# The last layer's tokens: 32x32 blocks and VectorE transposes in place of TensorE transposes

## The chip, the core and the metric

One core of one Trainium2 chip runs the whole program in one launch. The metric is the device time of an execution in microseconds (us); three executions of the kernel before were timed, and one more was taken by the hardware profiler.

## The reference

```
x = attention(q, k, v, beta)          # delta-rule state, 4 x 8 heads, 768 steps
x = moe(x, ...)                       # 3072 tokens, top-1 of 8 experts, D=384, F=1024
h = x @ w_in                          # 3072 x 384 by 384 x 2048
g = h * (1.0 / (1.0 + np.exp(-h)))
return (g @ w_out).astype(np.float32) # 2048 x 384
```

The change is in the last three lines, the dense layer ("Ffn" in the kernel). `w_in` and `w_out` arrive as 64-bit floats and are unpacked on the chip.

## The kernel before, in words

**Stages.** Attention and routing take about the first 310 us, the experts the next 220, the last layer the rest, from about 529 us of the span. The stages overlap at their edges: one scheduler puts the instructions of the whole program in order, engine by engine, by times that it works out itself; the code's `issue_after` gives it lower bounds. Each engine then runs its own list strictly in order, and SP's list holds nearly all DMAs.

**Experts (L1252, L1259).** The experts write their rows to a DRAM tensor `ys` (3072 x 384) by scatters from GpSimd. In the last slot of the experts each of eight pieces of the hidden dimension is a first product `ph` (nine matmuls), an activation that ScalarE writes and VectorE corrects (`pairs`, L1409 and L1410), and a second product `poe` of twelve matmuls: high by high, high by low, low by high, for four blocks of tokens. The weights of each piece are split into a high and a low part by ScalarE (L1215) and VectorE (L1216): `wRH` for the first product, `w2s` for the second.

**Last layer (`Ffn`).** Tokens are worked on in six groups of 512. `tokens(g)` (L1606) loads a group's 512 rows of `ys` into the tile `fy` (128 partitions, 4 blocks of 128 tokens, 384 features) by one DMA on SP (L1609), and turns them so that features lie on partitions: for each of three blocks k of 128 features, four TensorE transposes of 128x128 into one PSUM tile `fpt` (L1613), a cast to the high part `fxh` on ScalarE (L1614) and the low part `fxl` on VectorE (L1615). Two buffers of `fy` alternate; the second one, `fy2`, lies in memory that the experts' raw weights use until the last of them is split. `tokens(0)` is called in the experts' last slot, `tokens(g + 1)` in group g after its ninth piece.

`group(g)` (from L1618) goes through 16 pieces f of 128 hidden features: the first product `fph` (L1629, nine matmuls of 128x512), the sigmoid on ScalarE (L1632), the gated value gv on VectorE (L1634, written to a part of `fy2`'s memory, so the profile calls it fy), its high part gh on ScalarE (L1636, fgh) and its low part gl on VectorE (L1638, fq), and one piece later the second product `fpo` (L1646, twelve matmuls of 128x384). Within the first group the rest of `w_out` is still loaded (L1507, tiles `ro8` to `ro15`, two buffers) and unpacked by ScalarE and VectorE (L1518 to L1527). After 16 pieces the result goes out through `ob` (L1672, L1676).

PSUM has eight banks: five under the tag "pa", of which two hold the third and fourth block of a group's result and three go round between `fph` and `fpt`.

Of the kernel before, what the change touches and what calls it, by code (L numbers as in the profile page):

```python
# [715 lines left out]
class Router:  # L716
# [210 lines left out]
    def finish(self, n):  # L927
# [109 lines left out]
        def spots():  # L1037
            pd, ps = pick(self.pd), new("ps", [128, NT])
            if n == 0:
                u = tokens("u", v["w"], 2)  # L1040
                tt(ps, pd, u[:, 1], op=ALU.add)
                left = new("left", [128, NT])
                tt(left, pd, u[:, 0], op=ALU.is_ge)
                stt(ps, left, -1024.0, ps, op0=ALU.mult, op1=ALU.add)
            else:
                u = tokens("u", v["w"], 4)
                j, f = new("j", [128, NT]), new("f", [128, NT])
                tt(j, pd, u[:, 0], op=ALU.subtract)
                tt(ps, j, u[:, 2], op=ALU.add)
                tt(f, j, u[:, 1], op=ALU.is_ge)  # L1050
                tt(f, f, u[:, 3], op=ALU.mult)
                tt(ps, ps, f, op=ALU.add)
                nc.vector.tensor_scalar(f, j, 0.0, -1024.0, op0=ALU.is_lt, op1=ALU.mult)
                tt(ps, ps, f, op=ALU.add)
            v["ps"] = ps
# [475 lines left out]
class Ffn:  # L1531
# [74 lines left out]
    def tokens(self, g):  # L1606
        nc, P = self.nc, self.P
        xh, xl, y = self.take("xh"), self.take("xl"), self.take("y")
        nc.sync.dma_start(y, self.ys.rearrange("(t b p) d -> t p b d", b=4, p=128)[(g + 3) % 6])  # L1609
        for k in range(3):  # L1610
            pt = P["pa"].tile([128, 512], F32, tag="pa", name=f"fpt{g}_{k}")
            for c in range(4):
                nc.tensor.transpose(pt[:, 128 * c : 128 * c + 128], y[:, c, 128 * k : 128 * k + 128], self.ident)  # L1613
            nc.scalar.copy(xh[:, k, :], pt)  # L1614
            nc.vector.tensor_tensor(xl[:, k, :], pt, xh[:, k, :], op=ALU.subtract)  # L1615
        return xh, xl
# [222 lines left out]
```

## Time and profile before

| | before |
|---|---|
| median of 3 runs | 941.42 us (940.8 to 942.2) |
| the profiled execution | 947.22 us |
| its span, first to last instruction | 945.5 us |
| TensorE busy | 894.5 us, 95% |
| VectorE busy | 573.5 us, 61% |
| ScalarE busy | 429.3 us, 45% |
| DMA traffic | 85.27 MB in 68583 packets |

A row of the profile names a line of the kernel (L1613), an engine (PE is TensorE's matmul, PEld its weight load, DVE VectorE, ACT ScalarE, POOL GpSimd, SP the engine that issues DMAs), an operation and the tiles it writes and reads (out<-in). Busy times of TensorE's pipelined matmuls overlap a little, so the distance from one start to the next says more than a matmul's own duration. The profiled execution is longer than the median of the timed runs by 5.8 us.

### The profile page before, as it was taken

To read this page: it belongs to the slowest core of one execution; us is meant where nothing else is said; L and a number is where in the kernel's file an instruction comes from. 1 tells how busy PE (TensorE), PEld (TensorE's weight loads), DVE (VectorE), ACT (ScalarE), POOL (GpSimd) and SP (SyncE) were. 2 spreads that over 40 slices of the span, in tenths; PEclk is the share of its full clock that TensorE was granted. 3 is DMA by queue.
4 is the path that set the end of the run, shared out by engine and by line. 5 is a ranking of instruction groups with operands and counts; after the bars stand their busy time and mean duration, and the time that the engine had idled before them with its cause. 6 is when DMAs were issued, how large, how long until landed. Compare 5 with 4: busy or idle time off the path is not lost. (4 is left out here: it accounts for less than half of the span.)

```text
span 945.5 us, 23368 instructions
## 1 busy us (share of the span) xinstructions
PE 894.5 (95%) x9605; PEld 781.0 (83%) x9605; DVE 573.5 (61%) x1648; ACT 429.3 (45%) x842; POOL 83.7 (9%) x85
## 2 busy tenths in 40 slices
PE   7779998977999799999989999999999999999997
PEld 4449898876888577889878899898999999999997
DVE  4999898989924693699954556433333333343332
ACT  4127576853776434466643544333332332332332
POOL 5000000011011244122211100000000000000000
PEclk9897999988999999999999999999999999999999
DMA  8932746635154505576641312000010000000000
GB/s 199 176 102 73 171 106 167 163 86 185 34 142 116 176 22 171 172 233 197 214 145 58 104 50 68 34 2 33 34 34 1 34 1 1 34 1 1 34 0 34
DMA packets 68583, 85.27 MB, mean 90 GB/s; under 512 B 29961, under 2 KB 54679, under 8 KB 68464
## 3 DMA queue, kind: packets, MB, share of 16 engines
q1 hardware_dynamic: 65136, 73.83, 28.3%
q0 software_dynamic: 3328, 9.83, 3.1%
q8 instruction: 78, 1.28, 0.6%
q14 instruction: 41, 0.34, 0.1%
HBM read 70.53 MB, written 14.55 MB: 90 GB/s over the span
## 5 line engine op out<-in xcount | busy, mean ns | idle before, releaser
L1646 PE MATMUL fpo<-o,fgh 128*128 128x384 f32 x768 | 184.3, 338 | 0.0
L1634 DVE TENSOR_TENSOR fy<-fph,fy 128x512 f32<-128x512 f32 x96 | 66.4, 691 | 161.8 <-ACT fy L1632 161.3
L1646 PEld LDWEIGHTS fpo<-o,fgh 128*128 128x128 f32 x768 | 139.3, 188 | 7.9 <-ACT fgh L1636 0.4
L1632 ACT ACTIVATE fy<-fph 128x512 f32<-128x512 f32 x96 | 57.4, 598 | 169.4 <-PE fph L1629 166.6
L1646 PE MATMUL fpo<-o,fq 128*128 128x384 f32 x384 | 116.6, 338 | 0.0
L1629 PE MATMUL fph<-fxh,ih 128*128 128x512 f32 x288 | 113.7, 395 | 0.0
L1629 PE MATMUL fph<-fxh,il 128*128 128x512 f32 x288 | 113.2, 393 | 0.0
L1638 DVE TENSOR_TENSOR fq<-fy,fgh 128x512 fp32r<-128x512 f32 x96 | 66.4, 692 | 74.4 <-ACT fgh L1636 63.3
L1636 ACT CAST fgh<-fy 128x512 fp32r<-128x512 f32 x96 | 59.7, 622 | 80.4 <-DVE fy L1634 44.6
L1259 PE MATMUL poe<-w2s,pairs 128*128 128x384 f32 x384 | 77.5, 344 | 3.9 <-ACTq L1490 3.2
L1259 PEld LDWEIGHTS poe<-w2s,pairs 128*128 128x128 f32 x384 | 69.2, 191 | 8.0 <-ACTq L1490 3.5
L1646 PEld LDWEIGHTS fpo<-o,fq 128*128 128x128 f32 x384 | 71.1, 188 | 0.5
L416 DVE TENSOR_TENSOR tmp<-A,L 128x126 f32<-128x126 f32 (+20 forms) x336 | 70.7, 252 | 0.9
L422 DVE TENSOR_TENSOR A<-A,tmp 128x126 f32<-128x126 f32 (+20 forms) x336 | 70.5, 251 | 0.0
L1252 PE MATMUL bank<-xh,wRH 128*128 128x256 f32 x240 | 61.3, 332 | 6.6 <-DVE wRH L1308 6.0
L1629 PEld LDWEIGHTS fph<-fxh,il 128*128 128x128 f32 x288 | 54.1, 188 | 9.7
L1629 PEld LDWEIGHTS fph<-fxh,ih 128*128 128x128 f32 x288 | 54.1, 188 | 9.0
L1346 PE MATMUL po<-raw,hs 128*128 128x384 f32 x160 | 60.4, 501 | 0.0
L1629 PE MATMUL fph<-fq,ih 128*128 128x512 f32 x144 | 56.9, 395 | 0.0
L1629 PE MATMUL fph<-fxl,ih 128*128 128x512 f32 x144 | 56.5, 392 | 0.0
L1252 PEld LDWEIGHTS bank<-xh,wRH 128*128 128x128 f32 x240 | 41.6, 199 | 11.8 <-DVE wRH L1308 6.8
L709 PE MATMUL po<-ones 128*128 128x512 bf16 x103 | 32.9, 432 | 14.1 <-DVE KB L347 6.8
(432 smaller groups left out, 1587.2 us busy)
## 6 DMA issues: line engine op xcount, KB each, us to landing
raw<-in_moe_w_dram SPq DMA_DIRECT2D x72, 384.0 KB
ri<-in_moe_w_in_dram SPq DMA_DIRECT2D x12, 512.0 KB
ro<-in_moe_w_out_dram SPq DMA_DIRECT2D x16, 384.0 KB
vs<-in_vd_dram SPq DMA_DIRECT2D x12, 384.0 KB
KI<-in_kd_dram SPq DMA_DIRECT2D x24, 192.0 KB
Z<-vs SPq DMA_DIRECT2D x24, 192.0 KB
xs<-Y SPq DMA_DIRECT2D x48, 96.0 KB
fy<-ys SPq DMA_DIRECT2D x6, 768.0 KB
```

The lines of the kernel that those rows point to most:

```text
L416: nc.vector.tensor_tensor(tv, r[:, :, j : j + 1].to_broadcast([128, c, n]), L[:, j : j + 1, j + 1 :].to_broadcast([128, c, n]), op=ALU.mult,)
L422: nc.vector.tensor_tensor(r[:, :, j + 1 :], r[:, :, j + 1 :], tv, op=ALU.add)
L709: return nc.tensor.matmul(room, dense, dense[:, None, :].to_broadcast([128, 4, 128]), start=True, stop=True).ins
L1252: self.nc.tensor.matmul(ph, a[:, k, :], b[:, k, :], start=(i == 0), stop=(i == 8))
L1259: self.mark = self.nc.tensor.matmul(o, a[:, cs], b, start=(c == 0 and i == 0), stop=(c == self.F - 1 and i == 2)).ins
L1346: nc.tensor.matmul(self.po[b][:, 0:384], v["h"][c % 2][:, 128 * b : 128 * b + 128], self.raw(1, c), start=(c == 0), stop=(c == F - 1),)
L1629: nc.tensor.matmul(ph, a[:, k, fs], b[:, k, :], start=(n == 0), stop=(n == 8))
L1632: nc.scalar.activation(sg, ph, AF.Sigmoid)
L1634: nc.vector.tensor_tensor(gv, ph, sg, op=ALU.mult)
L1636: self.marks = [nc.scalar.copy(gh, gv).ins]
L1638: self.marks.append(nc.vector.tensor_tensor(gl, gv, gh, op=ALU.subtract).ins)
L1646: nc.tensor.matmul(po[c], a[:, rows], b, start=(f == 0 and i == 0), stop=(f == 15 and i == 2))
```

## The change

Only `tokens` changes. The one DMA of a group becomes twelve, for four ranges i of 32 features and three blocks k: each brings, for 32 partitions, 16 pieces of 32 floats, so that partition 32i + p holds, for each of 16 runs n of 32 tokens, 32 features of token 32n + p. A block transpose of 32x32 on VectorE then gives, in one instruction for each k, what four TensorE transposes gave. The casts that follow stay; their lines move from L1614 and L1615 to L1619 and L1620, and all later lines by 5.

```diff
     def tokens(self, g):
         nc, P = self.nc, self.P
         xh, xl, y = self.take("xh"), self.take("xl"), self.take("y")
-        nc.sync.dma_start(y, self.ys.rearrange("(t b p) d -> t p b d", b=4, p=128)[(g + 3) % 6])
+        blocks = self.ys.rearrange("(t n p) (k i d) -> t i p k n d", n=16, p=32, k=3, i=4)[(g + 3) % 6]
+        y = y.rearrange("p b d -> p (b d)").rearrange("p (k n) -> p k n", k=3)
+        for i in range(4):
+            for k in range(3):
+                nc.sync.dma_start(
+                    y[32 * i : 32 * i + 32, k].rearrange("p (n d) -> p n d", d=32), blocks[i, :, k]
+                )
         for k in range(3):
             pt = P["pa"].tile([128, 512], F32, tag="pa", name=f"fpt{g}_{k}")
-            for c in range(4):
-                nc.tensor.transpose(pt[:, 128 * c : 128 * c + 128], y[:, c, 128 * k : 128 * k + 128], self.ident)
+            nc.vector.transpose(out=pt, in_=y[:, k])
             nc.scalar.copy(xh[:, k, :], pt)
             nc.vector.tensor_tensor(xl[:, k, :], pt, xh[:, k, :], op=ALU.subtract)
         return xh, xl
```

The scheduler gives the new program another order in the last slot of the experts and in the last layer. VectorE, last slot of the experts (`wRH` and `w2s` are low parts of weights, `pairs` low parts of activations, the number in `ph_12_4` is the piece), as a difference:

```order
 L1216 TENSOR_TENSOR wRH<-raw_4193,wRH 128x384
+L1618 STREAM_TRANSPOSE fpt_0_12019<-fy 128x512
 L1410 SCALAR_TENSOR_TENSOR pairs<-ph_12_4_11908,pairs 128x512
-L1216 TENSOR_TENSOR w2s<-raw_4284,w2s 128x384
+L1618 STREAM_TRANSPOSE fpt_1_12023<-fy 128x512
+L1620 TENSOR_TENSOR fxl<-fpt_0_12019,fxh 128x512
+L1216 TENSOR_TENSOR w2s<-raw_4284,w2s 128x384
+L1618 STREAM_TRANSPOSE fpt_2_12027<-fy 128x512
+L1620 TENSOR_TENSOR fxl<-fpt_1_12023,fxh 128x512
 L1216 TENSOR_TENSOR wRH<-raw_4193,wRH 128x384
 L1410 SCALAR_TENSOR_TENSOR pairs<-ph_12_5_11943,pairs 128x512
```

The three transposes of the first group stand ahead of, or between, the pairs of pieces 4 and 5; before, VectorE's first work on these tokens stood behind the pairs of piece 6. On ScalarE the casts `fxh` move up in the same way, the second one ahead of a weight cast and the pairs of piece 5.

TensorE at the same place, in the changed program, with what each row waits for (Activation is ScalarE):

```order
L1259 MATMUL poe_12_7568<-w2s,pairs 128x384 [waits Activation_49]
L1259 MATMUL poe_12_7568<-w2s,pairs 128x384 [waits DVE_49]
L1259 MATMUL poe_13_7569<-w2s,pairs 128x384 x2
L1259 MATMUL poe_14_7570<-w2s,pairs 128x384 x2
L1259 MATMUL poe_15_7571<-w2s,pairs 128x384 x2
L1252 MATMUL ph_12_6_11976<-pairs,wRH 128x512 [waits DVE_49]
L1259 MATMUL poe_12_7568<-w2s,pairs 128x384 [waits DVE_49]
L1259 MATMUL poe_13_7569<-w2s,pairs 128x384
L1259 MATMUL poe_14_7570<-w2s,pairs 128x384
L1259 MATMUL poe_15_7571<-w2s,pairs 128x384
L1252 MATMUL ph_12_6_11976<-pairs,wRH 128x512 x6
L1259 MATMUL poe_12_7568<-w2s,pairs 128x384 [waits Activation_49]
```

The first eight `poe` matmuls of piece 4 use high activations; the row after the single `ph` is the first that needs the low pairs of piece 4. The last row begins piece 5 and needs its high pairs from ScalarE. Before, the order here was nearly the same, with the single `ph` later.

SP from the end of the experts to the sixth load of weights of the last layer, before and then in the changed program:

```order
L1609 DMA fy<-ys 128x4x384
L1609 DMA fy_12093<-ys 128x4x384
L1609 DMA fy<-ys 128x4x384
L1507 DMA ro_12141<-in_moe_w_out_dram 128x768
L1507 DMA ro_12205<-in_moe_w_out_dram 128x768
L1507 DMA ro_12269<-in_moe_w_out_dram 128x768
L1507 DMA ro_12333<-in_moe_w_out_dram 128x768
L1609 DMA fy_12093<-ys 128x4x384
```

```order
L1613 DMA fy<-ys 32x16x32 x24
L1613 DMA fy_12095<-ys 32x16x32 x12
L1507 DMA ro_12143<-in_moe_w_out_dram 128x768
L1507 DMA ro_12207<-in_moe_w_out_dram 128x768
L1507 DMA ro_12271<-in_moe_w_out_dram 128x768
L1613 DMA fy_12095<-ys 32x16x32 x4
L1507 DMA ro_12335<-in_moe_w_out_dram 128x768
L1613 DMA fy_12095<-ys 32x16x32 x8
L1507 DMA ro_12423<-in_moe_w_out_dram 128x768
L1507 DMA ro_12487<-in_moe_w_out_dram 128x768
```

Thirty-six loads stand ahead of the first `ro` (ro10) where three did: the first group's, then the third group's into the same buffer, which wait for the first group's transposes, then the second group's. The fourth group's loads now stand on both sides of ro13.

## Rows read from the trace of the kernel before

**Rows 1.** The page, busy time, share of the span and instructions by engine.
```profile
PE 894.5 (95%) x9605; PEld 781.0 (83%) x9605; DVE 573.5 (61%) x1648; ACT 429.3 (45%) x842; POOL 83.7 (9%) x85
```

**Rows 2.** The chain that ended last, share of the span by line.
```profile
by line: PE fpo L1646 21.4%; PE fph L1629 21.1%; PE poe L1259 1.9%; PE ph L1252 1.6%; PE fpt L1613 0.8%; DVE wRH L1216 0.1%; DVE ob L1672 0.1%; ACT wRH L1215 0.1%; DVEq L1834 0.0%; issue 0.0%; ACTq L1215 0.0%
```

**Rows 3.** Pieces of that chain: start us, us, what; at two places.
```profile
523.82 1.31 PE fpt L1613 x12
...
564.80 0.87 PE fpt L1613 x8
...
567.76 0.44 PE fpt L1613 x4
```

**Rows 4.** Stretches of 68 us, one group each: length, busy us (x).
```profile
529.00:597.00 68.00, 68.00 (x348) 61.77 (x348) 43.27 (x83) 31.68 (x56) 4.27 (x4) 1.00 0.20 64
597.00:665.00 68.00, 68.00 (x347) 61.49 (x346) 24.57 (x37) 21.69 (x37) 0.00 (x0) 1.00 0.07 24
```

**Rows 5.** The page, groups by line: busy, mean ns, idle before, releaser.
```profile
L1646 PE MATMUL fpo<-o,fgh 128*128 128x384 f32 x768 | 184.3, 338 | 0.0
L1634 DVE TENSOR_TENSOR fy<-fph,fy 128x512 f32<-128x512 f32 x96 | 66.4, 691 | 161.8 <-ACT fy L1632 161.3
```

**Rows 6.** Groups of VectorE, each shape apart: block transposes of the attention.
```profile
L361 DVE STREAM_TRANSPOSE L<-G 128x1024 f32<-128x1024 f32 x6 | 11.6, 1937 | 0.1
L379 DVE STREAM_TRANSPOSE nt<-nm 128x32 f32<-128x32 f32 x6 | 0.9, 154 | 0.0
```

**Rows 7.** SP in order of time: start us, us, what; first token load.
```profile
509.43 0.38 SPq L1609 DMA_DIRECT2D fy<-ys  x1
```

**Rows 8.** SP's small copies: two batches in order of time; issue ns min/median/max of all.
```profile
99.68 7.19 SPq L444 DMA_DIRECT2D KA<-G  x8
...
236.44 5.43 SPq L444 DMA_DIRECT2D KA<-G  x8
...
L444 SPq DMA_DIRECT2D KA<-G x40: 594/628/1749, 99.7 to 268.8; - x40
```

**Rows 9.** DMA from 237.8 to 244.2: GB/s in 40 slices, queue.
```profile
GB/s 106 137 137 30 66 146 135 63 41 140 139 89 23 133 139 112 10 118 142 130 15 88 142 137 43 58 141 138 71 139 131 132 87 0 0 0 5 7 10 4
...
q1 hardware_dynamic: 4224, 0.52, 53.6%
```

**Rows 10.** SP in order of time near the routing's loads.
```profile
33.37 0.40 SPq L785 DMA_DIRECT2D mi<-in_moe_modality_id_dram  x1
35.71 4.57 SPq L787 DMA_DIRECT2D bb<-n_moe_modality_bias_dram  x1
```

**Rows 11.** VectorE in order of time, last slot of the experts.
```profile
513.63 0.56 DVE L1216 TENSOR_TENSOR wRH<-raw,wRH 128x384 fp32r<-128x384 f32 x1 [0.84 <-ACT wRH L1215]
514.13 0.69 DVE L1410 SCALAR_TENSOR_TENSOR pairs<-ph,pairs 128x512 fp32r<-128x512 f32 x1
```

**Rows 12.** TensorE in order of time, same slot, poe of piece 4 and then ph.
```profile
517.79 2.28 PE L1259 MATMUL poe<-w2s,pairs 128*128 128x384 f32 x12
519.91 1.79 PE L1252 MATMUL ph<-pairs,wRH 128*128 128x512 f32 x7
```

**Rows 13.** ScalarE in order of time, same slot.
```profile
517.28 0.51 ACT L1215 CAST wRH<-raw 128x384 fp32r<-128x384 f32 x1 [0.65 <-PE ph L1252]
517.70 0.59 ACT L1409 ACTIVATE pairs<-ph 128x512 fp32r<-128x512 f32 x1
```

**Rows 14.** SP in order of time: first weight load of the last layer, ro10.
```profile
536.49 0.35 SPq L1507 DMA_DIRECT2D ro<-in_moe_w_out_dram  x1
```

**Rows 15.** VectorE in order of time, first group: unpacking and the gated value.
```profile
535.90 0.56 DVE L1523 SCALAR_TENSOR_TENSOR ro8e<-ro,ro8e 128x384 int32<-128x384 int32 x1 [0.61 <-ACT ro8e L1520]
...
546.22 0.35 DVE L1518 TENSOR_SCALAR ro10e<-ro 128x384 int32<-128x384 int32 x1
...
555.47 0.68 DVE L1634 TENSOR_TENSOR fy<-fph,fy 128x512 f32<-128x512 f32 x1
```

**Rows 16.** DMA queue from 510 to 514, today's first token load: packets, MB, share.
```profile
q1 hardware_dynamic: 528, 0.79, 65.3%
```

## The prediction

> **What bounds the kernel now.** I read the page first. TensorE is busy for 95% of the span [rows 1], and the chain that ended last, followed back through the last half of the run, is TensorE nearly all the way: its two products fpo (L1646) and fph (L1629) hold 42.5% of the span, and the transposes fpt (L1613) of the change hold 0.8% [rows 2]. Next I read the chain in order of time, to see whether those transposes stand in line or in a hole. They stand in line: twelve of them in one piece of 1.31 us at 523.82, in the last slot of the experts, for the first group; in the later groups eight in 0.87 us and four in 0.44 us, again 1.31 us, with a fpo product on each side [rows 3]. Then the table by stage: in the 68 us of one group TensorE is busy for 68.00 us, VectorE for 43.27 us in the first group (which still unpacks the last weights) and 24.57 us in a later one [rows 4]. Last, the waits: fpo has no idle time before it, while VectorE's L1634 idles 161.8 us for ScalarE's sigmoid, which itself waits for TensorE [rows 5]. So each microsecond taken off TensorE there comes off the end, as long as VectorE, ScalarE and the loads keep their lead.
>
> **What is removed.** Six groups of 1.31 us [rows 3] are 7.86 us of TensorE, all on the chain. 0.8% of 945.5 us [rows 2] is 7.6 us, the same within its rounding. The Trainium skill, page "VectorE: DVE Perf Modes", section "Rules for kernel authors", speaks against the edit: it gives a 128x128 transpose to TensorE when PSUM is its destination. By that rule nothing would be won. The rows decide here, because TensorE has no free time in these stages and VectorE has.
>
> **The transposes on VectorE.** The nearest rows are the block transposes of the attention: 154 ns for 128x32 and 1937 ns for 128x1024 [rows 6]. The line through them gives 154 + 480 x 1.797 = 1017 ns for 128x512; I take 1.02 us. They write to SBUF, the new one to PSUM; without a row for that I allow 0.6 to 2.0 us. Eighteen cost 18.4 us of VectorE, three or 3.1 us in a group, beside 24.7 us of idle time in the first group and over 43 us in the others [rows 4]. Inside a group each delays a gv or gl by at most about 1 us, and a gl is needed only one fph product later, about 2.1 us. I cost them at nothing there. Without that cover, each would put its 1.02 us on TensorE.
>
> **The loads.** Six DMAs become 72, each of 512 pieces of 128 bytes in a pattern of 16 by 32. The profile has this shape: the copies KA<-G, eight at a time, but between places of SBUF, where the new ones start in DRAM. Eight of them were issued in 5.43 us in the best batch and 7.19 us in another [rows 8]; with 0.63 us for the last one, that is 0.69 to 0.94 us from one to the next. In the best batch the traffic ends in slot 33 of 40, at 243.1, some 1.8 us after the last issue; with the receipt I take 2.2 us from issue to landing [rows 8, 9]. The lower bound of the spacing is what the packets themselves take: 53.6% of 16 engines over 6.4 us for 4224 packets is 13 ns each, 32 per engine, 0.42 us [rows 9]. A higher one is the load mi, 3072 pieces of 8 bytes out of DRAM (L785): the next DMA was held until 40.28, 6.5 us after mi's issue ended, which is 1.1 us per 512 pieces [rows 10]. The far bound is the packets of today's fy load: 65.3% of 16 engines over 4 us for 528 packets is 79 ns, or 2.5 us per 512 [rows 16]. I take 0.7 us, the nearest row in shape and size.
>
> **Where this is on the path: the first group.** The first load cannot start before 509.43, when it does today [rows 7], because it waits for a scatter. Today nobody feels its landing; the transposes stand at 523.82. In the new order VectorE's first transpose stands between the wRH of 513.63 and the pairs of 514.13 [rows 11], and VectorE stops there until the tenth load has landed: 509.43 + 9 x 0.7 + 2.2 = 517.9. Then come the transpose (518.9) and the pairs (0.69 us, 519.7). TensorE, in its new order, does eight poe products and one ph before it asks for these pairs: from 517.79, with 0.177 us per poe and 0.23 per ph [rows 12], at 519.4. It stops 0.3 us. The second stop is through ScalarE, where the second fxh cast now stands ahead of a weight cast and the next pairs: the second transpose ends at 520.6, then about 0.5 us for the fxh cast, 0.42 us from the weight cast to the pairs, 0.59 us for these [rows 13] and the hand-overs make 522.2, and TensorE is there at 519.7 + 4 x 0.177 + 6 x 0.23 = 521.8, so 0.4 us. Together with hand-overs I take **0.8 us**. Each 0.1 us of spacing moves it by 0.9 us: nothing below about 0.6, 3.0 us at 0.94, 4.4 us at 1.1.
>
> **The queue behind them.** SP now issues 36 loads ahead of the weights ro10 where it had three. The second dozen, for the third group, waits for the first transposes: 518.9 + 24 x 0.7 = 535.7. Today ro10 goes out at 536.49 [rows 14], when VectorE has released its buffer at 536.46 [rows 15], so nothing is lost; VectorE reads it at 546.22 [rows 15]. The load ro13 now stands behind four loads that wait for the second group's first transpose, just after the L1634 of 555.47 [rows 15]; at 0.7 us each it goes out near 560, long before its use. The outputs and later loads share an SP queue that is idle for tens of microseconds; nothing.
>
> **Sum.** 7.86 - 0.8 = 7.1 us. The profiled execution took 947.22 us for a span of 945.5, so it would become 940.1. It is 5.8 us above the median of the runs, 941.42; the same 7.1 us taken from that gives **934.3 us**.
>
> **The rivals.**
> - *Slow loads, still a gain.* The spacing is that of mi, 0.95 to 1.2 us, because the data come from DRAM. TensorE stops 3 to 5.3 us: 936.5 to 939. For it: mi's row is the only one of many small pieces out of DRAM. Against: part of that hold was other loads ahead of it. 13%.
> - *Slow loads, slower kernel.* At 1.3 us per load the tenth lands at 523.3 and TensorE stops 6.2 us. 36 loads end at 524.4 + 24 x 1.3 = 555.6, ro10 lands near 558, and VectorE, which by then wants it at 546.22 + 4.9 = 551.1, stops 7 us in the middle of the first group; TensorE has 2 to 3 us of cover there, so it loses another 4 to 5. The sum is 2 to 4 us slower, 943.5 to 945.5. It decides from about 1.2 us per load. For it: 79 ns per packet of the fy load [rows 16]; against: 8-byte packets out of DRAM went at 1.1 us per 512 at the worst. 7%. The Trainium skill, page "DMA: Bandwidth & Descriptors", section "Why small descriptors are slow (HBM only)", says that copies within SBUF are spared the penalty of small pieces and copies with HBM are not, which is this rival's mechanism; no row of this trace shows 128 bytes out of DRAM.
> - *The transposes take 2 us into PSUM.* The pairs and casts of the first group come 1 to 2 us later each and TensorE stops about 4 us: 937.5. Against: 1937 ns for twice the size. 5%.
> - *No gain.* The time between the matmuls only moves to another stop in each group: 941 to 942. Against: fpo has no idle time, and both engines it waits for have 25 us and more to spare. 5%.
>
> **How the numbers follow.** My forecast, with spacings of 0.45 to 0.94 us (933.4 to 936.5), has 70%. A run of this kernel can be told from no change at about 0.2%, 1.9 us, so "faster" is below 939.5 and "slower" above 943.3. Faster: 70 + 11 of the slow loads + 4 of the slow transposes = 85%. Same: 2 + 1 + 5 = 8%. Slower: 7%. The range for 8 in 10 starts at 932.9, all 7.86 us and some scatter of the runs (940.8 to 942.2), and goes to 938.8, which takes in most of the slow loads and the slow transposes.
>
> **What would show it.** Right: no L1613 on TensorE; six groups of about 67 us from fph to fph; a stop of TensorE of 0 to 3 us at poe near 519 to 522, released by VectorE or ScalarE; VectorE idle ahead of its first transpose, released by a fy load; transposes of about 1.0 us. Wrong: loads spaced over 1.0 us on SP, VectorE waiting for ro10 near 546, or gaps of TensorE inside later groups.

## The result and the profile after

| | before | after |
|---|---|---|
| median of the runs | 941.81 us (940.8 to 943.79, 4 runs) | 933.14 us (931.8 to 935.76, 4 runs) |
| ratio | | 0.9909, 95% interval 0.9881 to 0.9936 |
| the profiled execution, its span | 947.22, 945.5 us | 935.76, 934.0 us |
| TensorE busy | 894.5 us | 885.7 us |

The changed kernel is 8.7 us faster (941.81 - 933.14); the interval reaches from 6.0 to 11.2 us. Forecast were 934.3 us in a range of 932.9 to 938.8. The forecast held, and its sign too. Its sum was 7.86 - 0.8 = 7.1 us, so something over a microsecond is still to be placed.

The page of the changed kernel, busy time, share and instructions, and below it the chain that ended last, by line (it answers to [rows 1, 2]):

```profile
PE 885.7 (95%) x9533; PEld 773.2 (83%) x9533; DVE 585.6 (63%) x1666; ACT 430.2 (46%) x842; POOL 88.2 (9%) x85
```

```profile
by line: PE fpo L1651 21.7%; PE fph L1634 21.4%; PE poe L1259 2.0%; PE ph L1252 1.7%; issue 0.1%; DVE w2s L1216 0.1%; DVE ob L1677 0.1%; ACT wRH L1215 0.1%; DVEq L1839 0.0%; ACTq L1215 0.0%; DVEq L1216 0.0%; DVE wRH L1216 0.0%
```

The 72 transposes are off TensorE (9605 instructions became 9533), and the chain has no fpt any more. VectorE has 12.1 us more to do.

The same two stretches of 68 us as in [rows 4], then two groups of the page as in [rows 5]:

```profile
529.00:597.00 68.00, 68.00 (x341) 61.54 (x340) 46.01 (x88) 31.12 (x56) 4.60 (x4) 1.00 0.22 56
597.00:665.00 68.00, 68.00 (x342) 61.61 (x341) 28.14 (x42) 22.64 (x39) 0.00 (x0) 1.00 0.11 24
```

```profile
L1651 PE MATMUL fpo<-o,fgh 128*128 128x384 f32 x768 | 183.4, 338 | 0.0
L1639 DVE TENSOR_TENSOR fy<-fph,fy 128x512 f32<-128x512 f32 x96 | 66.4, 691 | 141.6 <-ACT fy L1637 141.1
```

TensorE is still busy for all of a group and waits for nothing. VectorE's work in a group rose from 43.27 to 46.01 and from 24.57 to 28.14 us, and the wait of its L1639 for ScalarE fell by 20.2 us, about the 12.1 us of new work and the 8.1 us by which this part of the program got shorter (the stretch below): on VectorE the transposes took idle time.

The new operations by tile: duration in ns min/median/max, first and last start; the transposes, then the loads on SP.

```profile
L1618 DVE STREAM_TRANSPOSE fpt<-fy x18: 717/726/728, 510.8 to 825.8; 128x512 f32<-128x512 f32 x18
...
L1613 SPq DMA_DIRECT2D fy<-ys x72: 302/487/1281, 502.7 to 693.8; - x72
```

A transpose takes 0.72 us where the forecast had 1.02, and the loads follow each other on SP every 0.53 us (the median distance of the first dozen) where it had 0.7.

VectorE and then TensorE in the experts' last slot, in order of time (start, us, what; in brackets an idle time and what ended it), at the place of the forecast's stop:

```profile
510.31 0.56 DVE L1216 TENSOR_TENSOR wRH<-raw,wRH 128x384 fp32r<-128x384 f32 x1 [0.84 <-ACT wRH L1215]
510.79 0.72 DVE L1618 STREAM_TRANSPOSE fpt<-fy 128x512 f32<-128x512 f32 x1
511.42 0.67 DVE L1410 SCALAR_TENSOR_TENSOR pairs<-ph,pairs 128x512 fp32r<-128x512 f32 x1
```

```profile
514.46 1.58 PE L1259 MATMUL poe<-w2s,pairs 128*128 128x384 f32 x8
515.88 0.39 PE L1252 MATMUL ph<-pairs,wRH 128*128 128x512 f32 x1
516.10 0.87 PE L1259 MATMUL poe<-w2s,pairs 128*128 128x384 f32 x4
516.81 1.56 PE L1252 MATMUL ph<-pairs,wRH 128*128 128x512 f32 x6
```

No row has a bracket behind the wRH: the tokens were there, and TensorE asked for the low pairs at 516.10, four microseconds after VectorE had finished them. The forecast's stop of 0.8 us did not take place.

**A stretch that repeats.** Whole executions scatter by several microseconds, so I compare one stretch: from the first poe product of the fourth piece of the experts' last slot (piece 3, as pieces are numbered from 0; up to there TensorE has the same work in both programs, and the order first differs one piece later) to the start of the last fpo product. The table holds all kernels of this study. "Stop" is the time in which TensorE stood still inside the stretch (gaps over 0.1 us in the rows of its matmuls; their ends are modelled, so a short stop can hide); "first load" and "first transpose" are starts, counted from the start of the stretch.

| kernel | stretch starts | stretch, us | stop, us | first load | first transpose |
|---|---|---|---|---|---|
| before | 513.35 | 426.92 | 0 | -3.92 | |
| after | 510.03 | 418.78 | 0 | -7.33 | 0.75 |
| after_again | 510.04 | 418.78 | 0 | -3.37 | 4.05 |
| loads_only | 509.53 | 426.92 | 0 | -6.79 | |
| turns_only | 506.18 | 418.78 | 0 | -5.02 | 0.75 |
| first_only | 507.59 | 425.66 | 0 | -3.53 | 3.80 |
| later_only | 512.92 | 420.03 | 0 | -7.35 | |
| loads_x2 | 512.68 | 419.50 | 0.17 | -7.28 | 4.92 |
| loads_x3 | 514.87 | 429.19 | 8.15 | -4.72 | 13.03 |
| turns_x3 | 513.20 | 424.45 | 2.73 | -3.30 | 3.95 |
| turns_sbuf | 512.05 | 419.27 | 0 | -3.97 | 3.32 |
| loads_x3_by_k | 513.28 | 430.02 | 4.17 + 3.85 | -4.73 | 3.49 |
| before_again | 510.84 | 426.92 | 0 | -6.96 | |

The change is worth 426.92 - 418.78 = 8.14 us, 0.86% of the run, and that lies in the interval of the timed runs. The other 3.3 us between the two profiled executions (513.35 against 510.03) arose ahead of anything the change touches on TensorE; they are also most of the 4.3 us by which the profiled execution (935.76) beat its forecast of 940.1.

### The profile page after: what moved, and what is told of

The parts are those of the page before. It is cut to its first block, busy times and chain, and to the rows that moved or that the text cites. A ratio compares the mean times of both kernels' runs of the same rounds, so it can differ in the third digit from the quotient of the medians.

```text
span 934.0 us, 23350 instructions
## 1 busy us (share of the span) xinstructions
PE 885.7 (95%) x9533; PEld 773.2 (83%) x9533; DVE 585.6 (63%) x1666; ACT 430.2 (46%) x842; POOL 88.2 (9%) x85
## 3 DMA queue, kind: packets, MB, share of 16 engines
q8 instruction: 77, 1.26, 0.6%
## 5 line engine op out<-in xcount | busy, mean ns | idle before, releaser
L1639 DVE TENSOR_TENSOR fy<-fph,fy 128x512 f32<-128x512 f32 x96 | 66.4, 691 | 141.6 <-ACT fy L1637 141.1
L1220 POOL DMA_INDIRECT xg<-xs,gidx x26 | 32.8, 1260 | 151.8 <-PE bank L1234 96.1
```

Of the source, the lines that this page charges most:

```text
L1220: self.nc.gpsimd.indirect_dma_start(out=rows, out_offset=None, in_=self.xs[0 : self.xs.shape[0] // (2 - n), :], in_offset=bass.IndirectOff ...
L1639: nc.vector.tensor_tensor(gv, ph, sg, op=ALU.mult)
```

## The experiments

**The changed kernel again.** No edit.

> The changed kernel as it is, five rounds. Theory (chain): the gain is the TensorE time of the 72 transposes, 6 x 1.31 = 7.86 us, with no stop in the first group, so 7.9 us less than before (ratio 0.9916); groups are about 1.3 us shorter each. Rival (the order upstream): the profiled runs stood 3.3 us apart already at the same poe products ahead of the first token load, so part of the measured 8.7 us is won earlier in the program; then the interval lies wholly beyond 8.2 us and the place 3 us ahead of the change shows again.

Ratio 0.9899, interval 0.9869 to 0.9928; stretch 418.78 again. The interval holds 8.14 us as well as 9.5, so the time alone doesn't decide, and the stretch does. The rival's second sign did appear: the stretch began at 510.04, 3.3 us earlier than in the first profile of the kernel before. But that kernel's second profile, next, began at 510.84, so such a place isn't the change's doing. This execution also tests the stop, because its first load came 4 us later against TensorE than in the first profile. VectorE and then TensorE:

```profile
514.08 0.73 DVE L1618 STREAM_TRANSPOSE fpt<-fy 128x512 f32<-128x512 f32 x1 [3.21 <-DMA fy<-ys]
514.72 0.67 DVE L1410 SCALAR_TENSOR_TENSOR pairs<-ph,pairs 128x512 fp32r<-128x512 f32 x1
```

```profile
515.88 0.39 PE L1252 MATMUL ph<-pairs,wRH 128*128 128x512 f32 x1
516.11 0.87 PE L1259 MATMUL poe<-w2s,pairs 128*128 128x384 f32 x4
```

VectorE stood for 3.21 us for the tenth load, as the forecast described it, and still ended the pairs at 515.4, 0.7 us ahead of TensorE's question at 516.11. The wait is real, and it is hidden.

**The kernel before again.** No edit.

> The kernel before, profiled once more. Theory (the last part of the program repeats to the hundredth, the scatter of whole runs is made ahead of it): stretch 426.92 us again, five groups of 68.2 to 68.5 us, while the place of the first token load in the program moves by a microsecond or more. Rival: the stretch itself scatters by a microsecond, and the 8.14 us between the profiles is partly chance.

The stretch is 426.92 to the hundredth; its start moved by 2.5 us, as much as the two executions differ (947.22 and 944.73 us), and the first load moved by 3 us against it. So the theory holds: between these two executions the scatter comes from ahead of the stretch.

**The loads without the transposes.**

```diff
-            nc.vector.transpose(out=pt, in_=y[:, k])
+            for c in range(4):
+                nc.tensor.transpose(pt[:, 128 * c : 128 * c + 128], y[:, k, 128 * c : 128 * c + 128], self.ident)
```

> The twelve block loads stay, the TensorE transposes come back; they read blocks of 32x32 in an arrangement that needs another turn, so the last layer works on other values, with the same work. Theory (chain): the loads alone cost nothing, TensorE has its 6 x 1.31 us again: within 1 us of before, TensorE busy as before, no stop at the first group. Rival (slow loads eat part of the gain): slower than before by 1 us or more, with TensorE or VectorE waiting for a load or for ro10.

Ratio 0.9999 (0.9975 to 1.0023), stretch 426.92: sixty-six more DMAs cost nothing here. The order that the scheduler made for it has the transposes later, so this prices the traffic and SP's time, not the waits of the changed order.

**The transposes without the loads.**

```diff
-        for i in range(4):
-            for k in range(3):
-                nc.sync.dma_start(
-                    y[32 * i : 32 * i + 32, k].rearrange("p (n d) -> p n d", d=32), blocks[i, :, k]
-                )
+        nc.sync.dma_start(y, self.ys.rearrange("(t b p) d -> t p b d", b=4, p=128)[(g + 3) % 6])
```

(with the load ahead of the new view of `y`)

> One load of whole rows per group as before, VectorE transposes as after; they turn blocks within the row arrangement, so the last layer works on other values, with the same work. Theory (chain): the whole gain without the loads: 7.9 us less than before, and equal to the changed kernel within 0.7 us, since its loads are hidden. Rival (slow loads): 1 us or more faster than the changed kernel, because loads hold its first group back.

Ratio 0.9895 (0.9861 to 0.9929), stretch 418.78: the changed kernel's own. Its loads hide entirely. The order on TensorE is the changed kernel's, so here the waits are tested too.

**The first group alone, and the others alone.** `tokens(g)` of the kernel before is kept as `tokens_old`; in the second kernel the condition is `g == 0`:

```diff
+        if g > 0:
+            return self.tokens_old(g)
```

> Block loads and VectorE transposes in the first group alone, the other five groups as before. Theory (chain): 1.31 us less than before if TensorE doesn't stop in the experts' last slot; the forecast's stop of 0.8 us would leave 0.5 us. Rival (the first group wins more, by its loads or its order): 2.5 us or more less than before.

> The first group's tokens as before (one load, TensorE transposes), the other five as in the changed kernel. Stretch: from the first poe product of the fourth piece of the experts' last slot to the last fpo product, 426.92 us before and 418.78 us after, the same in both profiles of the changed kernel. Theory (chain): five sets of transposes go, the stretch is 426.92 - 5 x 1.36 = 420.1 us, the time about 6.8 us less than before. Rival (the first group wins more by its order): 418.5 to 419.5.

The first group alone: ratio 0.9972 (0.9945 to 0.9998), stretch 1.26 us shorter. The others alone: 0.9938 (0.9912 to 0.9963), 6.89 us shorter. 1.26 + 6.89 = 8.15: every group gives its share, and neither a gain nor a loss is peculiar to the first. (6.89 is 5 x 1.31 and some 0.3 us at the end of the last group, placed further down.)

**Each load cut in two, then in three.**

```diff
-                nc.sync.dma_start(
-                    y[32 * i : 32 * i + 32, k].rearrange("p (n d) -> p n d", d=32), blocks[i, :, k]
-                )
+                for a, b in ((0, 16), (16, 32)):
+                    nc.sync.dma_start(
+                        y[32 * i : 32 * i + 32, k].rearrange("p (n d) -> p n d", d=32)[:, :, a:b],
+                        blocks[i, :, k, :, a:b],
+                    )
```

and with the ranges (0, 16), (16, 24), (24, 32) for three.

> Each block load of the changed kernel cut into two of half the width (24 loads per group, pieces of 64 bytes). Theory (issue bound: 0.53 us from load to load on SP, whatever the width): the 20th load lands 19 x 0.53 + 2.2 = 12.3 us after the first is issued, the first transpose and the pairs end 1.4 us later, 13.7, and TensorE wants them 13.4 us after the first load (516.1 - 502.7 in the changed kernel), so it stops 0.3 us there and up to 1.2 us behind it: stretch 419.1 to 420.3 us. Rival (small pieces out of DRAM cost by the piece): a stop of 5 us or more.

> Each block load cut into three (64, 32 and 32 bytes wide; 36 loads per group). Theory (issue bound, 0.53 us each): the 30th lands 29 x 0.53 + 2.2 = 17.6 us after the first is issued, the pairs are done at 19.0 where TensorE wants them at 13.4: a stop of 5.6 us and up to 1 us behind it, stretch 424.4 to 425.4 us; the order puts 77 loads ahead of ro10, which then lands about when VectorE wants it. Rival (queue): ro10 lands late as well and TensorE stops in the first group too, stretch above 428. Rival (the loads are hidden anyway): stretch below 421.

With two, ratio 0.992 (0.9892 to 0.9949) and a stretch of 419.50, 0.7 us above the changed kernel's. VectorE's first transpose, and TensorE behind it:

```profile
517.61 0.73 DVE L1620 STREAM_TRANSPOSE fpt<-fy 128x512 f32<-128x512 f32 x1 [4.09 <-DMA fy<-ys]
```

```profile
518.53 0.39 PE L1252 MATMUL ph<-pairs,wRH 128*128 128x512 f32 x1
518.96 0.96 PE L1259 MATMUL poe<-w2s,pairs 128*128 128x384 f32 x4
519.76 1.55 PE L1252 MATMUL ph<-pairs,wRH 128*128 128x512 f32 x6
521.48 1.66 PE L1259 MATMUL poe<-w2s,pairs 128*128 128x384 f32 x8 [0.17 <-ACT pairs L1409]
```

Here are the two stops that the forecast named. One ph takes 0.23 us of TensorE, and 0.43 pass from 518.53 to the poe that needs the low pairs (0.2 us too much, shown as no gap because the ends of matmuls are modelled); the second stop, one piece later, is released by ScalarE's pairs. Start to start the two stops take 0.2 and 0.3 us, and the poe behind each another 0.1, which makes the 0.7. The mechanism was right, and it begins at about 1.06 us per block (2 x 0.53) with an early first load. In the first group VectorE also waits a little for ro10, as the forecast's second rival had it, but TensorE shows no gap there:

```profile
545.07 0.36 DVE L1518 TENSOR_SCALAR ro10e<-ro 128x384 int32<-128x384 int32 x1 [0.79 <-DMA ro<-in_moe_w_out_dram]
```

With three, ratio 1.0029 (1.0001 to 1.0058) and a stretch of 429.19, 2.3 us above the kernel before: slower, by little. TensorE, then two rows of the table by stretches (length, busy us of PE, PEld, DVE, ACT, POOL, granted clock, DMA share, GB/s):

```profile
520.72 0.39 PE L1252 MATMUL ph<-pairs,wRH 128*128 128x512 f32 x1
529.26 1.65 PE L1259 MATMUL poe<-w2s,pairs 128*128 128x384 f32 x4 [8.15 <-DVE pairs L1410]
530.70 2.76 PE L1252 MATMUL ph<-pairs,wRH 128*128 128x512 f32 x6
```

```profile
515.00:521.00 6.00, 6.00 (x32) 5.28 (x30) 0.56 (x1) 0.62 (x2) 0.00 (x0) 1.00 0.60 42
...
529.20:533.20 4.00, 3.94 (x10) 3.43 (x11) 3.81 (x8) 2.95 (x7) 0.00 (x0) 0.50 0.58 45
```

The first transpose came 17.75 us after the first load, as expected (17.6). I had put TensorE's question at 13.4 us after the first load, from the profile of the changed kernel; but in this execution the first load stood 2.6 us nearer to TensorE's place (-4.72 against -7.33), so the stop was 8.15 in place of 5.6 us. And it cost 10.41 us of the stretch, not 8.15: in the 4 us behind it the granted clock was 0.50, the lower of its two levels (1.2 in place of 2.4 GHz), and four poe took 1.44 us and six ph 2.56 (start to start) where the changed kernel has 0.71 and 1.40. The stop that the queue's rival expected from ro10 did not come. With 77 loads ahead of it ro10 went out at 552.39, 37.5 us into the stretch where the changed kernel has 21.9, but VectorE, held up by the first stop, read it at 556.13 without waiting, and no gap of TensorE stands in the first group.

**The narrow loads in another order.** The loop over k outside the loop over i, else as with three.

> The 36 narrow loads of a group again, but all those of the first block of features go first, then the second, then the third; the order on VectorE and TensorE is that of the run with 36 loads. Theory (each transpose waits in VectorE's queue for its own loads, with everything behind it): the first transpose starts about 12 loads x 0.53 + 2 us = 8.4 us after the first load in place of 17.7 us, so the stop of 8.15 us ahead of the low pairs of piece 4 goes; the second and third transpose still wait for the 24th and 36th load, ahead of the next pairs, so TensorE stops 3 us or more one piece later: stretch 424 to 429 us. Rival (only the first transpose was on the path): stretch 419 to 421 us.

One execution: stretch 430.02, 1 us above the theory's range, far from the rival's 421. VectorE:

```profile
516.78 0.73 DVE L1620 STREAM_TRANSPOSE fpt<-fy 128x512 f32<-128x512 f32 x1 [2.66 <-DMA fy<-ys]
517.41 0.67 DVE L1410 SCALAR_TENSOR_TENSOR pairs<-ph,pairs 128x512 fp32r<-128x512 f32 x1
523.49 0.73 DVE L1620 STREAM_TRANSPOSE fpt<-fy 128x512 f32<-128x512 f32 x1 [5.41 <-DMA fy<-ys]
...
531.22 0.73 DVE L1620 STREAM_TRANSPOSE fpt<-fy 128x512 f32<-128x512 f32 x1 [5.97 <-DMA fy<-ys]
```

The first transpose is 9.5 us earlier, and the stop only moves: TensorE now stands 4.17 us behind the second one (for ScalarE's pairs, which queue behind the cast of that transpose) and 3.85 us behind the third (for a fxl that VectorE has behind it):

```profile
525.80 2.93 PE L1259 MATMUL poe<-w2s,pairs 128*128 128x384 f32 x8 [4.17 <-ACT pairs L1409]
532.58 2.07 PE L1252 MATMUL ph<-pairs,wRH 128*128 128x512 f32 x4 [3.85 <-DVE fxl L1622]
```

The stretch is 11.24 us longer than the changed kernel's, the stops are 8.02. Most of the rest is the clock again: from 526.00 to 528.50 and from 533.00 to 535.00 the granted clock was 0.50, and the poe followed each other at about 0.32 us in place of 0.18. What counts is when the last load of the group lands, because work that TensorE needs queues behind each transpose.

**Each transpose three times.**

```diff
-            nc.vector.transpose(out=pt, in_=y[:, k])
+            for _ in range(3):
+                nc.vector.transpose(out=pt, in_=y[:, k])
```

> Each VectorE transpose done three times over (54 in place of 18). Theory (VectorE's spare time covers them): 36 more transposes of 0.72 us are 26 us of VectorE, nothing in the later groups (66.9 to 67.3 us each as in the changed kernel), 0 to 2 us in the experts' last slot, stretch 418.8 to 420.8 us. Rival (a transpose delays gv and gl and so TensorE): groups longer by up to 6 x 0.72 = 4.3 us, stretch 430 or more.

Ratio 0.9969 (0.9948 to 0.9989), stretch 424.45: neither. From fpo to fpo the groups after the first took 67.1 to 67.4 us where the changed kernel has 66.9 to 67.3, so 0.1 to 0.2 us for six more transposes: covered, as the theory said. The other 5 us are a stop ahead of the first fpo and a slow clock behind it. ScalarE, then TensorE:

```profile
531.69 2.00 ACT L1434 ACTIVATE ysb<-poe,gate 128x384 f32<-128x384 f32 x4 [3.53 <-PE poe L1259]
533.71 1.28 ACT L1638 ACT_TABLE_LOAD   x1
535.00 1.08 ACT L1638 ACTIVATE fy<-fph 128x512 f32<-128x512 f32 x2
```

```profile
537.03 1.95 PE L1652 MATMUL fpo<-o,fgh 128*128 128x384 f32 x8 [2.73 <-ACT fgh L1642]
```

With more VectorE work the scheduler made another order. On ScalarE all four writes of the experts' rows (ysb), which wait for the last poe, now stand ahead of the load of the sigmoid's table, the first sigmoids and the cast that the first fpo needs, while TensorE has only seven fph products left and then waits. In the profile of the changed kernel the table load stands 5 us ahead of the first of these writes:

```profile
523.22 1.28 ACT L1637 ACT_TABLE_LOAD   x1
...
528.28 0.58 ACT L1434 ACTIVATE ysb<-poe,gate 128x384 f32<-128x384 f32 x1 [0.91 <-PE poe L1259]
```

In turns_x3 the granted clock was again 0.50 from 539.00 to 541.40. The miss belongs to this order; that the transposes themselves would cost more in the first slot was not shown.

**The destination of the transposes.** In groups two to six:

```diff
-            pt = P["pa"].tile([128, 512], F32, tag="pa", name=f"fpt{g}_{k}")
+            if g:
+                pt = self.take("sg")
+            else:
+                pt = P["pa"].tile([128, 512], F32, tag="pa", name=f"fpt{g}_{k}")
```

> In groups two to six the VectorE transposes write to the sigmoid's buffers in SBUF in place of a PSUM tile; the casts read them there. It prices the destination. Theory of the forecast (the line through the attention's transposes, which write to SBUF): 1.02 us per transpose into SBUF against 0.72 us into PSUM. Rival (128x512 costs 0.7 us wherever it goes, and the line was too steep): 0.70 to 0.75 us. Either way the time stays within 1 us of the changed kernel, the stretch at 418.8 to 419.8 us, since VectorE has room.

Ratio 0.993 (0.9895 to 0.9965), stretch 419.27. VectorE by shape (busy, mean ns, idle before):

```profile
L361 DVE STREAM_TRANSPOSE L<-G 128x1024 f32<-128x1024 f32 x6 | 11.7, 1945 | 0.1
L1621 DVE STREAM_TRANSPOSE fy<-fy 128x512 f32<-128x512 f32 x15 | 10.7, 711 | 0.4
L1621 DVE STREAM_TRANSPOSE fpt<-fy 128x512 f32<-128x512 f32 x3 | 2.2, 721 | 2.5 <-DMA fy<-ys 2.5
```

0.71 us into SBUF and 0.72 into PSUM: the rival. The destination doesn't matter at this size; the line through 128x32 and 128x1024 was too steep at 512.

## Why the prediction was right

- **What bounds the kernel: right.** TensorE's chain lost the transposes and the end came forward by as much. turns_only and loads_only split it: all with the transposes, nothing with the loads.
- **"Six groups of 1.31 us are 7.86 us": right.** Start to start, the 72 transposes hold 6.96 us of TensorE in the profile before, 0.097 each. The matmul right behind each of their eleven groups starts its successor 0.084 us late, 0.92 us in all; in the changed kernel none does. Together that is 7.88 us. Why a matmul lags behind a transpose was not tried.
- **Not in the sum: a stop at the end, 0.3 us.** The rest of the 8.14 us stands in the last group, which has no transposes. There the last product of the kernel before waits for ScalarE's fgh, and that of the changed kernel doesn't. TensorE's weight loads (PEld), before and then after:

```profile
938.26 1.34 PEld L1646 LDWEIGHTS fpo<-o,fgh 128*128 128x128 f32 x8 [0.36 <-ACT fgh L1636]
```

```profile
926.73 1.40 PEld L1651 LDWEIGHTS fpo<-o,fgh 128*128 128x128 f32 x8
```

  Two matmuls there start their successors 0.31 us late in all. The order of this group is the scheduler's, and turns_sbuf, with all its transposes on VectorE, has the same stop (0.36 us at 929.31, of the 0.5 us by which its stretch is longer). So this part of the gain goes with the order and not with the transposes as such; for the forecast it was luck.
- **The stop of 0.8 us: not there.** This is the step that failed, in its sizes. The spacing of 0.7 us was 0.53, near the lower bound of 0.42 [rows 9] rather than the nearest row in shape [rows 8]; the tenth load was issued 4.64 us behind the first where I had 6.3. The transpose of 1.02 us holds up the next row by 0.64. Against them the landing took 2.8 us (after_again: the tenth load issued 4.64 - 3.37 = 1.27 us into the stretch, the transpose at 4.05) where I had 2.2, and the first load came 0.55 us later (-3.37 where the profile before has -3.92). The balance turns a stop of 0.3 us into 0.7 us of margin. The second stop isn't there either: in after_again ScalarE's pairs end 7.64 us into the stretch, and the poe that needs them starts at 8.18. Also "the first load cannot start before 509.43" was one draw: it stood 3.3 to 7.4 us ahead of the stretch in thirteen profiles, and the scatter that it waits for moves too. With the 0.8 us that did not come and the 0.3 us of the last group, the forecast's 7.1 us become the 8.14 of the stretch, within 0.1.
- **The transposes at no cost inside a group: right.** Tripled, they cost at most 0.2 us per group.
- **The queue: right, with room.** On SP in the profile after (start, us, what), which answers to [rows 7, 14], the 36 loads end at 528.77 and ro10 goes out 3 us later, when its buffer is free:

```profile
502.70 26.07 SPq L1613 DMA_DIRECT2D fy<-ys  x36
531.92 15.59 SPq L1507 DMA_DIRECT2D ro<-in_moe_w_out_dram  x3
```

  That VectorE waits for ro10 when the loads take longer was seen in loads_x2 (0.79 us), without a stop of TensorE; loads_x3 became slower through the first stop instead.
- **The rival of slow loads, slower kernel:** its outcome came at 1.59 us per block (three loads of 0.53), by the first of the two stops that it named (8.15 us where it had 6.2, and a slow clock behind) and without the second, for ro10. Its cause, small pieces out of DRAM being dear, is not there. The 79 ns that spoke for it belong to packets of 1.5 KB (0.79 MB in 528 [rows 16]). In 6.3 us from 511.5 of the profile after, DMA queue:

```profile
q1 hardware_dynamic: 5128, 0.64, 64.6%
```

  0.646 x 16 x 6.3 / 5128 is 12.7 ns per packet of 128 bytes out of DRAM, what the copies inside SBUF took (13 ns) [rows 9]. The Trainium skill, page "DMA: Bandwidth & Descriptors", section "Why small descriptors are slow (HBM only)", would have copies from HBM suffer alone; at 128 bytes the trace doesn't show it.
- **The other rivals: wrong.** Loads came every 0.53 us, not 0.95 or more, and a transpose into PSUM took 0.72 us, not 2. The gain didn't move to another stop: turns_only has the whole of it. The Trainium skill, page "VectorE: DVE Perf Modes", section "Rules for kernel authors", gives a 128x128 transpose to TensorE when PSUM is its destination. Here, where TensorE is the bound and VectorE idles, the measurement decides the other way: 8.14 us less with the transposes on VectorE.
- **"Can be told from no change at about 0.2%": too hopeful.** Five rounds of this kernel gave intervals of 0.2 to 0.35% to each side, since a run of before lay anywhere from 937.4 to 950.2 us in the first batch of runs. The forecast of 934.3 against 933.14 is within that; its nearness says less than the stretch does.

By the stretch no kernel of the study beats the changed one: it has no stop of TensorE left in the stretch that its tokens could remove.

## What to carry to other kernels

Where the chain is one engine without gaps, take work off it and count start to start, with the lag of the instruction behind; even 72 DMAs in place of 6 cost nothing here, as they start early enough. Check the one place where the new work stands in an in-order queue ahead of something the bound engine wants soon, and ask when the last of the loads lands. If whole runs scatter by more than the gain, compare a stretch that repeats between two marks of the trace.

## What the runs showed of the hardware

- SP issued a load of 512 pieces every 0.53 us, whether the pieces had 128, 64 or 32 bytes (loads_x2 and loads_x3 have the same median distance).
- A block transpose of 128x512 took 0.71 us and one of 128x1024 1.94 us, 2.7 times as much for twice the elements; why was not tried.
- The stops of TensorE of some microseconds cost more than themselves: behind 8.15 us the granted clock was 0.50 for 4 us (2.3 us lost), behind 4.17 us (loads_x3_by_k) and 2.73 us (turns_x3) it fell to 0.50 too, while behind the stops of 0.2 and 0.3 us in loads_x2 it stayed at 1.00.
- The matmul right behind a group of TensorE transposes started its successor 0.084 us late, eleven times out of eleven in the profile before; why was not tried.
